# A gated scan and a routed expert layer on one core: scan rounds and matmul units in turns, sums of squares on TensorE, streamed expert weights

## The chip, the cores and the metric

The kernel runs on one core of a Trainium2 chip. The metric is the time of one execution in microseconds (us) on the device; the median of several runs is compared.

## What is computed

The reference has two parts. The first is a gated linear recurrence for 4 batches x 8 heads, 768 steps, head size 48, with a complex state of 48 x 48 per head:

```python
mag = np.sqrt(a_re * a_re + a_im * a_im)
scale = np.minimum(mag, 0.999) / (mag + 1e-06)
...
for t in range(S):
    new_re = ar * S_re - ai * S_im
    new_im = ar * S_im + ai * S_re
    S_re, S_im = (new_re + k_t v_t^T, new_im)
    y[:, :, t] = q_t S_re
```

Its output, 3072 rows of 384, is the input of the second: a layer of 8 experts where each row goes to the one expert with the largest logit (`x @ w_gate` plus a bias by modality), and is scaled by that expert's probability:

```python
h = np.maximum(x[mask] @ w1[e], 0.0)            # 384 -> 1024
out[mask] = gate_w[mask, None] * (h @ w2[e])    # 1024 -> 384
```

## The kernel before

The 768 steps are cut into 8 blocks of 96 steps. Batch, head and block together are 256 chains; 128 of them lie on the 128 partitions, so there are two **rounds** (two batches each).

`elem(r)` scans a round on VectorE, backwards in time, in 12 chunks of 8 steps. `A` holds the products of the gates from a step to the block's end; a step is two dependent instructions, `x<-A,an` (L132) and `A<-x` (L135). `norm` makes the gates `an` of a chunk: squares on ScalarE (L63), their sum on VectorE (`m`, L66), logarithm and exponentials on ScalarE, then `g` (L73) and `an` (L76) on VectorE. `hats` divides by the products: squares of `A` (L90), their sum on VectorE (`me`, L93), logarithm and exponential, then `qc`, `Qh` and `A*kc` on VectorE; `Qh` is turned by TensorE (`tq`, L107) into `QT`, and the scaled keys go to DRAM as `kh`. Both are generators whose pieces are written between the steps of the scan. `A` and `QT` have one buffer each.

`units(r)` has 16 units, 8 blocks x 2 batches. A unit loads `kh` and `v` (from ScalarE's DMA queue), turns the keys (`tk`, L170), multiplies them with `QT` (`wp`, L176), masks the product on VectorE (`KW`, L177), and makes state and output (`py`, L191 and L195). From block 1 on, the state of the block before is first multiplied by the block's decay (`t1`, `t2`, `Z`, L154 to L157, both batches at once). Then come the router's logits (`lg_ps`, L204), and the output goes as bfloat16 rows to DRAM (`x_rows`).

The program runs `elem(0)`, `units(0)`, `elem(1)`, `units(1)`, in this order of writing. Each engine has one in-order queue; the framework's scheduler sets its order when the kernel is built, and may move an instruction ahead where its inputs and buffers are ready.

`moe_sorted` then casts all weights to bfloat16 into SBUF (16 DMAs on POOL's queue, L253 and L254), makes the routing (logits, largest, rank within the expert, position in a list of slots: a chain on VectorE, with 64 small matmuls into `inv_ps`, L370), and runs 31 slot tiles of 128 rows. A tile belongs to one expert, whose number is read into a register of TensorE (`texp`). It gathers its rows (`xg`, indirect DMA on POOL's queue), turns them (`xg_ps`, L386), multiplies up (`h_ps`, L395, 24 matmuls), applies the rectifier on VectorE and ScalarE (`hT`), multiplies down (`y_ps`, L403, 8 matmuls), scales (`y_sb`) and scatters (`out_dram`, L406). The lines where the register stands in an address:

```python
te = nc.values_load(texp[0:1, i:i + 1], engines=[ET.PE], min_val=0, max_val=E - 1, ...)
...
nc.tensor.matmul(h_ps[:, f, :], w1s[:, bass.ds(te, 1), k, ff * 128:(ff + 1) * 128], xgT[:, k, :], ...)
...
nc.tensor.matmul(y_ps[:], hT[:, f, :], w2s[:, bass.ds(te, 1), f, :], ...)
```

Of the kernel before, what the change touches and what calls it, by code (L numbers as in the profile page):

```python
# [22 lines left out]
def gate_loop(nc, ctx, tc, cpool, ident, identb, q, k, v, a_re, a_im, wgp, x_rows, lg):  # L23
# [10 lines left out]
    T = 8  # L34

# [12 lines left out]
    def rows(x, r):  # L48
        return x[r * NB:(r + 1) * NB].rearrange("b h (g t) d -> (b h g) t d", t=L)

    def planes(x, n):
        return x[:, None].broadcast_to([P, 2, n, D])

    for_round = []

    def norm(r, c, box):

        t0 = c * T
        ab = st.tile([P, 2, T, D], F32, name="ab")
        nc.sync.dma_start(out=ab[:, 0], in_=rows(a_re, r)[:, t0:t0 + T])  # L60
        nc.sync.dma_start(out=ab[:, 1], in_=rows(a_im, r)[:, t0:t0 + T])
# [12 lines left out]
        yield  # L74
        an = st.tile([P, T, 4, D], F32, name="an", bufs=3)
        nc.vector.tensor_tensor(an[:, :, 0:2, :].rearrange("p t c d -> p c t d"), ab[:], planes(g, T), Alu.mult)  # L76
# [4 lines left out]
    def hats(r, c, A, QT):  # L81

        t0 = c * T
        qc = st.tile([P, T, D], F32, name="qc")
        kc = st.tile([P, T, D], F32, name="kc")
        nc.sync.dma_start(out=qc[:], in_=rows(q, r)[:, t0:t0 + T])
        nc.sync.dma_start(out=kc[:], in_=rows(k, r)[:, t0:t0 + T])
        e = A[:, t0 + 1:t0 + T + 1]
        sq = st.tile([P, T, 2, D], F32, name="sqe", tag="sq")
        nc.scalar.activation(sq[:], e, Act.Square)  # L90
# [9 lines left out]
        nc.vector.tensor_tensor(Qh[:], e, qc[:, :, None, :].broadcast_to([P, T, 2, D]), Alu.mult)  # L100
        yield
        nc.vector.tensor_tensor(e, e, kc[:, :, None, :].broadcast_to([P, T, 2, D]), Alu.mult)
        nc.sync.dma_start(out=kh[r, :, t0:t0 + T], in_=e.rearrange("p t c d -> p t (c d)"))
        for t4 in range(0, T, 4):
            tp = ps.tile([C, 4, P], F32, name="tq", tag="tp", bufs=2)
            for i in range(4):
                nc.tensor.transpose(tp[:, i, :], Qh[:, t4 + i].rearrange("p c d -> p (c d)"), ident[:])  # L107
            nc.scalar.copy(QT[:, :, t0 + t4:t0 + t4 + 4], tp.rearrange("c t p -> c p t"))  # L108

    def elem(r):  # L110
        A = qt.tile([P, L + 1, 2, D], F32, name="A")
        QT = qt.tile([C, P, L], F32, name="QT")
        for_round.append(QT)
        nc.vector.memset(A[:, L, 0, :], 1.0)
        nc.vector.memset(A[:, L, 1, :], 0.0)
        box = {}
        last = L // T - 1
        for c in (last, last - 1):
            for _ in norm(r, c, box):
                pass  # L120
        for c in range(last, -2, -1):

            hs = hats(r, c + 1, A, QT) if c < last else iter(())
            ns = norm(r, c - 2, box) if c > 1 else iter(())
            beside = [ns, hs, ns, hs, hs, ns, hs, hs, ns]
            next(ns, None)
            next(hs, None)
            if c >= 0:
                an = box.pop(c)
                for t in range(c * T + T - 1, c * T - 1, -1):  # L130
                    x = st.tile([P, 2, 2, D], F32, name="x")
                    nc.vector.tensor_tensor(x[:], A[:, t + 1, :, None, :].broadcast_to([P, 2, 2, D]), an[:, t - c * T].rearrange("p (u w) d -> p u w d", u=2), Alu.mult)  # L132
                    if beside:
                        next(beside.pop(0), None)
                    nc.vector.tensor_tensor(A[:, t], x[:, 0], x[:, 1], Alu.add)  # L135
            for g in (ns, hs):
                for _ in g:
                    pass
        nc.sync.dma_start(out=c_scr[r], in_=A[:, 0].rearrange("p c d -> p (c d)"))

    def units(r):
        QT = for_round[r]
        khv = kh[r].rearrange("(b h g) t c -> b g t h c", h=H, g=G)
        cv = c_scr[r].rearrange("(j u g) c -> u g j c", u=2, g=G)
        state = None
        for g in range(G):
            if g:
                cB = un.tile([P, NB * J, 2, D], F32, name="cB")
                for u in range(2):
                    nc.scalar.dma_start(out=cB[u * 64:(u + 1) * 64].rearrange("p j c d -> p j (c d)"), in_=cv[u, g][None].broadcast_to([64, NB * J, C]))  # L150
                t1 = un.tile([P, NB * J, 2, D], F32, name="t1", bufs=1)
                t2 = un.tile([P, NB * J, 2, D], F32, name="t2", bufs=1)
                Z = un.tile([P, NB * J, 2, D], F32, name="Z", bufs=1)
                nc.vector.tensor_tensor(t1[:], state[:], cB[:, :, 0:1, :].broadcast_to([P, NB * J, 2, D]), Alu.mult)  # L154
# [67 lines left out]
    for r in range(NR):  # L222
        units(r)
        if r + 1 < NR:
            elem(r + 1)
# [252 lines left out]
```

## Time and profile before

| what | before |
|---|---|
| runs, median of 3 | 863.29 us (860.55 to 863.85) |
| profiled execution | 852.87 us |
| its span, first to last instruction | 851.2 us |
| mean granted TensorE clock | 0.735 |
| TensorE busy | 581.7 us (68%) |
| VectorE busy | 360.2 us (42%) |
| ScalarE busy | 280.2 us (33%) |
| GpSimd (POOL) busy | 82.8 us (10%) |
| DMA, bytes and mean rate | 71.58 MB, 84 GB/s |

A busy time is the union of an engine's instructions. TensorE's matmuls are pipelined, so a busy TensorE may still wait inside; the distance from one matmul to the next tells more. PE is TensorE's matmuls, PEld its loads of the stationary operand, PEclk the share of the full clock that was granted (1.00 or 0.50 in any one moment). In the first 130 us the clock column shows 1.00 although the distances between matmuls are those of the low level; the distances are used there. A DMA share over 1 stands for engines that were full all the time.

### The profile page before, as it was taken

How to read it: one execution, taken by the hardware profiler on the slowest of the kernel's cores; microseconds unless marked ns; L12 is line 12 of the kernel's file. 1: busy time of each engine (PE TensorE's matmuls, PEld its weight loads, DVE VectorE, ACT ScalarE, POOL GpSimd, SP SyncE). 2: the span in 40 equal slices, each digit the busy share in tenths (PEclk: the TensorE clock that was granted, in tenths of full speed). 3: DMA queues.
4: the chain of work that ended last, by engine and by line, in shares of the span. 5: the costliest groups of instructions: out<-in, count | busy, mean ns of one | idle time of the engine just before them, and what ended most of it. 6: DMA issues, size and time to landing. Idle time of an engine off the chain costs nothing. (4 is left out here: it accounts for less than half of the span.)

```text
span 851.2 us, 11577 instructions
## 1 busy us (share of the span) xinstructions
PE 581.7 (68%) x3599; PEld 367.9 (43%) x3599; DVE 360.2 (42%) x835; ACT 280.2 (33%) x620; POOL 82.8 (10%) x122
## 2 busy tenths in 40 slices
PE   0122128998889712299998930179999999999996
PEld 0121125766666512166776720164444444444443
DVE  5999971256767999523334320700111101111110
ACT  6766542253645874333434310001111111111111
POOL 0000000000000000000000032021212212122110
PEclk9999999967977955567879975555665656566665
DMA  4434343342532542433334169960110101111000
GB/s 140 140 116 144 111 132 85 69 105 68 130 105 86 160 146 90 118 79 78 82 77 95 29 94 207 208 115 29 33 39 29 42 29 33 39 29 42 11 1 1
DMA packets 104774, 71.58 MB, mean 84 GB/s; under 512 B 72878, under 2 KB 96930, under 8 KB 104720
## 3 DMA queue, kind: packets, MB, share of 16 engines
q0 software_dynamic: 14992, 20.36, 11.8%
q1 hardware_dynamic: 24768, 30.82, 11.8%
q10 hardware_dynamic: 64960, 19.67, 10.5%
q8 instruction: 35, 0.57, 0.3%
q14 instruction: 19, 0.16, 0.1%
HBM read 66.79 MB, written 17.99 MB: 100 GB/s over the span
## 5 line engine op out<-in xcount | busy, mean ns | idle before, releaser
L395 PE MATMUL h_ps<-xgT,w1s 128*128 128x128 bf16 x744 | 169.5, 250 | 20.2 <-DVE xgT L388 14.5
L107 PE MATMUL tq<-ident,Qh 128*96 128x128 f32 x192 | 42.6, 397 | 151.7 <-DVE Qh L100 150.9
L395 PEld LDWEIGHTS <-w1s 128*128 x744 | 76.5, 103 | 118.0 <-issue 42.9
L107 PEld LDWEIGHTS tq<-ident,Qh 128*96 128x96 f32 x192 | 32.3, 184 | 161.2 <-issue 78.9
L400 ACT ACTIVATE hT<-h_ps 128x512 bf16<-128x512 f32 x31 | 18.5, 597 | 236.1 <-PE h_ps L395 236.1
L191 PE MATMUL py<-KW,V 96*64 96x192 f32 x512 | 82.3, 405 | 7.4 <-issue 7.3
L177 DVE TENSOR_TENSOR KW<-wp,mask 96x384 f32<-96x384 f32 x64 | 35.3, 553 | 120.3 <-PE wp L176 119.2
L403 PE MATMUL y_ps<-w2s,hT 128*128 x248 | 83.8, 515 | 0.0
L388 DVE COPY xgT<-xg_ps 128x384 bf16<-128x384 bf16 x31 | 11.1, 358 | 150.6 <-PE xg_ps L386 150.6
L176 PE MATMUL wp<-QT,KT 96*96 96x96 f32 x512 | 72.0, 305 | 2.1 <-ACT KT L171 1.9
L132 DVE TENSOR_TENSOR x<-A,an 128x192 f32<-128x192 f32 x192 | 68.2, 355 | 6.1 <-ACT an L78 1.8
L176 PEld LDWEIGHTS wp<-QT,KT 96*96 96x96 f32 x512 | 64.0, 212 | 12.2 <-ACT KT L171 5.4
L398 DVE TENSOR_SCALAR hT<-h_ps 128x512 bf16<-128x512 f32 x31 | 21.5, 692 | 91.8 <-PE h_ps L395 91.8
L164 POOL MEMSET V<- 96x128 f32 x32 | 6.4, 202 | 466.1 <-PE py L191 466.1
L135 DVE TENSOR_TENSOR A<-x 128x96 f32<-128x96 f32 x192 | 49.1, 255 | 4.4
L382 POOL DMA_INDIRECT xg<-x_rows,idg x31 | 30.3, 976 | 204.5 <-PE xg_ps L386 172.5
L403 PEld LDWEIGHTS <-hT 128*128 128x128 bf16 x248 | 35.1, 146 | 31.9 <-issue 31.3
L170 PE MATMUL tk<-ident,KW 96*96 96x96 f32 x256 | 40.3, 298 | 10.9 <-DMA KW<-kh 10.5
L191 PEld LDWEIGHTS py<-KW,V 96*64 96x64 f32 x512 | 39.5, 167 | 18.5 <-issue 15.1
L195 PE MATMUL py<-QT,Zs 96*48 96x96 f32 x448 | 47.4, 285 | 0.0
L108 ACT COPY QT<-tq 96x512 f32<-96x512 f32 x48 | 27.5, 583 | 47.0 <-PE tq L107 44.0
L201 ACT COPY yT<-py 128x192 f32<-128x192 f32 x64 | 20.5, 320 | 65.9 <-DVE state L200 60.9
(115 smaller groups left out, 745.5 us busy)
## 6 DMA issues: line engine op xcount, KB each, us to landing
kh<-A SPq DMA_DIRECT2D x24, 384.0 KB, 2.9
KW<-kh ACTq DMA_DIRECT2D x32, 288.0 KB, 3.2
w1s<-in_moe_w_dram POOLq DMA_DIRECT2D x8, 768.0 KB, 27.5
w2s<-in_moe_w_dram POOLq DMA_DIRECT2D x8, 768.0 KB
cB<-c_scr ACTq DMA_DIRECT2D x28, 192.0 KB, 3.8
ab<-in_a_re_dram SPq DMA_DIRECT2D x24, 192.0 KB, 2.4
V<-in_v_dram ACTq DMA_DIRECT2D x32, 144.0 KB, 2.9
ab<-in_a_im_dram SPq DMA_DIRECT2D x24, 192.0 KB, 2.5
```

Source lines behind the costliest of these rows:

```text
L107: nc.tensor.transpose(tp[:, i, :], Qh[:, t4 + i].rearrange("p c d -> p (c d)"), ident[:])
L108: nc.scalar.copy(QT[:, :, t0 + t4:t0 + t4 + 4], tp.rearrange("c t p -> c p t"))
L132: nc.vector.tensor_tensor(x[:], A[:, t + 1, :, None, :].broadcast_to([P, 2, 2, D]), an[:, t - c * T].rearrange("p (u w) d -> p u w d", u=2 ...
L135: nc.vector.tensor_tensor(A[:, t], x[:, 0], x[:, 1], Alu.add)
L170: nc.tensor.transpose(tp[:, i, :], KW[:, h4 + i, 0:C], ident[:L, :L])
L176: nc.tensor.matmul(wp[:, i, :], KT[:, h4 + i, :], QT[:, p, :], start=True, stop=True)
L177: nc.vector.tensor_tensor(KW[:, h4:h4 + 4, C:], wp[:], mask[:, None, :].broadcast_to([L, 4, L]), Alu.mult)
L191: nc.tensor.matmul(py[u * 64:(u + 1) * 64, i, :], V[:, 2 * j + u, :], KW[:, 2 * j + u, :], start=True, stop=(g == 0))
L195: nc.tensor.matmul(py[u * 64:u * 64 + D, i, C:], Zs[:, j, u * 64:u * 64 + D], QT[:, p, :], start=False, stop=True)
L382: nc.gpsimd.indirect_dma_start(out=xg[:], out_offset=None, in_=x_rows_dram, in_offset=bass.IndirectOffsetOnAxis(ap=idg[:, i:i + 1], axis=0))
L395: nc.tensor.matmul(h_ps[:, f, :], w1s[:, bass.ds(te, 1), k, ff * 128:(ff + 1) * 128], xgT[:, k, :], start=(k == 0), stop=(k == KD - 1))
L403: nc.tensor.matmul(y_ps[:], hT[:, f, :], w2s[:, bass.ds(te, 1), f, :], start=(f == 0), stop=(f == NF - 1))
```

## The change

- **Scan.** The products are kept per chunk (`e`, three buffers) in place of the whole of `A`; `QT` has two buffers. `total` adds the two planes of squares on TensorE, by two float32 matmuls with the identity into the same PSUM tile, and ScalarE's logarithm reads PSUM: VectorE's `m` and `me` are gone. `norm` is cut into `modulus` and `gates`.
- **Turns.** `elem` and `units` are generators; the 13 turns of `elem(1)` are written between the 16 units of `units(0)`. A unit's first half (`front`) is written ahead of the second half (`back`) of the unit before.
- **Units.** `wp` is made in two halves of 64 output rows; the logits go to four column groups and are added by a matmul with `pairsum`; the decay is done per batch; the DMAs of a unit are issued from SP.
- **Weights.** 16 cast DMAs on POOL's queue bring the weights as bfloat16 to DRAM (`w1b`, `w2b`), one per turn of the scan, each waiting for that turn's last step.
- **Experts.** 19 slot tiles of 256 rows. SP reads the expert's number and streams its weights into one of three buffers; TensorE's addresses are fixed. The next tile's transposes stand between the up and the down part. The scatters no longer wait for each other.

```diff
+    def total(x, y):
+        out = ps.tile([P, T, D], F32, name="total", tag="wp", bufs=2)
+        nc.tensor.matmul(out[:], ident[:], x, start=True, stop=False)
+        nc.tensor.matmul(out[:], ident[:], y, start=False, stop=True)
+        return out[:]
...
-        nc.vector.tensor_tensor(m[:], sq[:, 0], sq[:, 1], Alu.add)
-        nc.scalar.activation(m[:], m[:], Act.Ln, scale=1.0 / (0.999 * 0.999))
+        nc.scalar.activation(m[:], total(sq[:, 0], sq[:, 1]), Act.Ln, scale=1.0 / (0.999 * 0.999))
...
-        nc.vector.tensor_tensor(m[:], sq[:, :, 0], sq[:, :, 1], Alu.add)
-        nc.scalar.activation(m[:], m[:], Act.Ln)
+        nc.scalar.activation(m[:], total(sq[:, :, 0], sq[:, :, 1]), Act.Ln)
...
-        QT = qt.tile([C, P, L], F32, name="QT")
+        QT = qt.tile([C, P, L], F32, name="QT", bufs=2)
...
+                if casts and (r or c < last - 1):
+                    cast = casts.pop(0)()
+                    tc.add_manual_dep(cast.ins, done.ins.name, ...)
...
-                        nc.tensor.matmul(wp[:, i, :], KT[:, h4 + i, :], QT[:, p, :], start=True, stop=True)
+                    for u in range(2):
+                        nc.tensor.matmul(wp[u * 64:(u + 1) * 64, i, :], KT[:, h4 + i, u * 64:(u + 1) * 64], QT[:, p, :], start=True, stop=True)
...
-                    nc.tensor.matmul(lg_ps[:, b, :], wgp[:, j, :], yT[:, j, :], start=(j == 0), stop=(j == J - 1))
+                nc.tensor.matmul(lg_ps[j * 32:(j + 1) * 32, b, :], wgp[:, j, :], yT[:, j, :], start=True, stop=True)
...
-    elem(0)
-    for r in range(NR):
-        units(r)
-        if r + 1 < NR:
-            elem(r + 1)
+    for _ in elem(0):
+        pass
+    for r in range(NR):
+        us = units(r)
+        if r + 1 < NR:
+            es = elem(r + 1)
+            n, m = NB * G, NCH + 1
+            done = 0
+            next(es)
+            for i in range(n):
+                next(us)
+                while done * n < (i + 1) * (m - 1):
+                    next(es)
+                    done += 1
...
+    def fetch(i):
+        te = nc.values_load(texp[0:1, i:i + 1], engines=[ET.SP], min_val=0, max_val=E - 1, ...)
+        w1t = fp.tile([128, KD, F], BF16, name="w1t")
+        w2t = fp.tile([128, NF, Dt], BF16, name="w2t")
+        nc.sync.dma_start(out=w1t[:], in_=w1b[bass.ds(te, 1)].rearrange("e p k f -> p (e k) f"))
+        nc.sync.dma_start(out=w2t[:], in_=w2b[bass.ds(te, 1)].rearrange("e p c d -> p (e c) d"))
...
+                    nc.tensor.matmul(h_ps[:, f, :], w1t[:, k, ff * 128:(ff + 1) * 128], xgT[:, k, :], start=(k == 0), stop=(k == KD - 1))
...
+                nc.tensor.matmul(y_ps[:], hT[:, f, s * 128:(s + 1) * 128], w2t[:, f, :], start=(f == 0), stop=(f == NF - 1))
...
+            tc.declare_no_dep(sc.ins, group="scatter", reason="rows of different tokens")
...
+    got = fetch(0)
+    xgT = turn(got[2])
     for i in range(NS):
+        coming = fetch(i + 1) if i + 1 < NS else None
+        hT = up(got[0], xgT)
+        if coming:
+            xgT = turn(coming[2])
+        down(i, got[1], hT)
+        got = coming
```

How the change moves instructions shows at three places. First TensorE's queue where one expert tile ends and the next begins (ISA is a register operation); before:

```order
L403 LDWEIGHTS hT
L403 ISA
L403 MATMUL y_ps<-w2s,hT 128x384
L386 LDWEIGHTS xg
L386 MATMUL xg_ps<-identb,xg 128x128
L383 TENSOR_LOAD texp
L395 ISA
L395 LDWEIGHTS w1s
L395 ISA
L395 MATMUL h_ps<-xgT,w1s 128x128
```

and in the change, where an up part ends, with the transposes of the next tile and the first down matmul (one of each kind):

```order
L477 LDWEIGHTS w1t
L477 MATMUL h_ps<-xgT,w1t 128x256
L465 LDWEIGHTS xg
L465 MATMUL xg_ps<-identb,xg 128x128
L489 LDWEIGHTS hT
L489 MATMUL y_ps<-w2t,hT 128x384
```

The read of the expert's number and the register operations are gone from this queue, and a matmul into `h_ps` has 256 columns.

Second VectorE's queue in the middle of round 0's units, where `state` and `Z` are the units' and the others the scan's; before:

```order
L132 TENSOR_TENSOR x<-A,an 128x192
L135 TENSOR_TENSOR A<-x 128x96
L177 TENSOR_TENSOR KW<-wp,mask 96x4x96 x2
L73 SCALAR_TENSOR_TENSOR g<-m,g 128x384
L200 TENSOR_TENSOR state<-Z,py 128x192
L97 TENSOR_TENSOR qc<-qc,me 128x384
L76 TENSOR_TENSOR an<-ab,g 128x2x8x48
L200 TENSOR_TENSOR state<-Z,py 128x192
L100 TENSOR_TENSOR Qh<-A,qc 128x768
L177 TENSOR_TENSOR KW<-wp,mask 96x4x96
L102 TENSOR_TENSOR A<-A,kc 128x768
L66 TENSOR_TENSOR m<-sq 128x384
```

and in the change:

```order
L155 TENSOR_TENSOR e<-x 128x96
L237 TENSOR_TENSOR state<-Z,py 128x192
L148 TENSOR_TENSOR x<-e,an 128x192
L237 TENSOR_TENSOR state<-Z,py 128x192
L109 TENSOR_TENSOR qc<-qc,me 128x384
L206 TENSOR_TENSOR t_1655<-state,cB 128x384
L112 TENSOR_TENSOR Qh<-e,qc 128x768
L207 TENSOR_TENSOR t_1656<-state,cB 128x384
L119 TENSOR_TENSOR e<-e,kc 128x768
L208 TENSOR_TENSOR Z<-t_1655,t_1656 128x4x48
```

Here `state` stands between the two halves of a step of the scan, which queues behind `py` on TensorE. The last step of the second scan stands behind 14 of the 16 units of round 0; before, six of its chunks stood behind the last unit.

Third POOL's queue around the routing (`io`, `idp`, `pref` are constants that the routing reads); before:

```order
L253 DMA w1s<-in_moe_w_dram 128x3x1024
L254 DMA w2s<-in_moe_w_dram 128x8x384
L258 IOTA io_4339 128x128
L260 IOTA idp_4341 96x32
L262 IOTA pref 96x8
L275 AFFINE_SELECT trib<-trib 128x128
L320 IOTA thr 128x24
L382 DMA xg<-x_rows,idg 128x384 x6
```

and in the change:

```order
L182 MEMSET KT 96x8x32
L179 MEMSET V 96x8x16 x2
L331 IOTA io_4901 128x128
L333 IOTA idp_4903 96x32
L335 IOTA pref 96x8
L337 IOTA thr 128x12
L348 AFFINE_SELECT trib<-trib 96x96
L457 DMA xg<-x_rows,idg 128x384 x10
L496 DMA out_dram<-y_sb,ids 3072x384 x2
```

The casts stand far ahead, eleven of them before the first unit's mask and five between the units' memsets.

## Rows read from the trace of the kernel before

**Rows 1.** Windows: start:end, length, busy PE PEld DVE ACT POOL, clock, DMA share, GB/s.

```profile
0.00:130.00 130.00, 23.04 (x97) 17.55 (x98) 109.73 (x285) 75.68 (x135) 1.36 (x10) 1.00 0.44 133
130.00:285.00 155.00, 140.49 (x1123) 104.59 (x1124) 86.61 (x195) 73.92 (x196) 3.23 (x16) 0.85 0.36 89
285.00:361.00 76.00, 20.68 (x106) 15.54 (x104) 65.32 (x164) 42.72 (x81) 0.00 (x0) 0.56 0.45 133
361.00:498.00 137.00, 126.26 (x1128) 95.42 (x1126) 46.22 (x84) 50.93 (x146) 2.63 (x13) 0.83 0.30 71
498.00:570.00 72.00, 15.02 (x69) 14.15 (x69) 20.09 (x47) 0.42 (x1) 17.40 (x25) 0.50 1.07 178
570.00:846.00 276.00, 256.18 (x1082) 120.68 (x1082) 32.19 (x61) 36.44 (x62) 57.19 (x58) 0.61 0.10 28
```

**Rows 2.** Timeline of one expert tile, TensorE: start, length in us, line, operation, count.

```profile
649.86 5.73 PE L395 MATMUL h_ps<-xgT,w1s 128*128 128x128 bf16 x24 [0.45 <-DVE xgT L388]
655.39 0.42 PE L386 MATMUL xg_ps<-identb,xg 128*128 128x128 bf16 x2
655.60 2.76 PE L403 MATMUL y_ps<-w2s,hT 128*128 x8
```

**Rows 3.** Windows of two short stretches, for their clock (columns as in rows 1).

```profile
655.60:658.40 2.80, 2.80 (x11) 1.32 (x10) 0.00 (x0) 0.60 (x1) 0.00 (x0) 0.50 0.00 0
...
407.40:409.10 1.70, 1.70 (x21) 1.70 (x22) 0.59 (x2) 0.66 (x2) 0.00 (x0) 1.00 0.46 115
```

**Rows 4.** Line 395: TensorE's sequencer, durations in ns (min/median/max).

```profile
L395 PEldq FUSED_REGOPS  x1488: 46/55/60, 569.8 to 842.5; - x186
```

**Rows 5.** Timeline, TensorE: the same 16 passes of wp in two units.

```profile
362.15 2.88 PE L176 MATMUL wp<-QT,KT 96*96 96x96 f32 x16
...
407.47 1.55 PE L176 MATMUL wp<-QT,KT 96*96 96x96 f32 x16
```

**Rows 6.** The page's DMA part: mean rate; the SP queue (packets, MB, share of 16 engines).

```profile
DMA packets 104774, 71.58 MB, mean 84 GB/s; under 512 B 72878, under 2 KB 96930, under 8 KB 104720
...
q1 hardware_dynamic: 24768, 30.82, 11.8%
```

**Rows 7.** Timeline of the routing, VectorE and POOL; in brackets the idle time before.

```profile
534.80 0.49 DVE L302 SCALAR_TENSOR_TENSOR cand<-sh,pref 96x256 f32<-96x256 f32 x1 [24.42 <-POOL pref L262]
...
565.87 1.04 POOL L382 DMA_INDIRECT xg<-x_rows,idg  x1 [30.75 <-DVE empty L376]
567.21 0.98 POOL L382 DMA_INDIRECT xg<-x_rows,idg  x1 [0.30 <-issue]
```

**Rows 8.** Groups by line, TensorE: count, then busy us and mean ns of one.

```profile
L191 PE MATMUL py<-KW,V 96*64 96x192 f32 x512 | 82.3, 405 | 7.4 <-issue 7.3
L176 PE MATMUL wp<-QT,KT 96*96 96x96 f32 x512 | 72.0, 305 | 2.1 <-ACT KT L171 1.9
...
L204 PE MATMUL lg_ps<-yT,wgp 128*8 128x96 f32 x256 | 37.7, 280 | 4.0 <-ACT yT L201 3.0
```

**Rows 9.** Timeline of the first scan, VectorE: first and last step, and two adds' neighbours.

```profile
12.78 0.26 DVE L135 TENSOR_TENSOR A<-x 128x96 f32<-128x96 f32 x1
...
17.30 0.56 DVE L66 TENSOR_TENSOR m<-sq 128x384 f32<-128x384 f32 x1
17.78 0.55 DVE L73 SCALAR_TENSOR_TENSOR g<-m,g 128x384 f32<-128x384 f32 x1
...
118.26 0.26 DVE L135 TENSOR_TENSOR A<-x 128x96 f32<-128x96 f32 x1
```

**Rows 10.** Timeline, TensorE: last transposes of the first scan, first of the units.

```profile
122.86 1.91 PE L107 MATMUL tq<-ident,Qh 128*96 128x128 f32 x8 [6.33 <-DVE Qh L100]
...
129.92 1.49 PE L170 MATMUL tk<-ident,KW 96*96 96x96 f32 x8 [5.14 <-DMA KW<-kh]
```

**Rows 11.** Window of the casts (columns as in rows 1).

```profile
499.00:537.00 38.00, 0.63 (x2) 0.18 (x2) 5.09 (x16) 0.42 (x1) 14.18 (x21) 0.50 1.18 193
```

**Rows 12.** Timeline, TensorE: the last two matmuls.

```profile
844.63 0.84 PE L403 MATMUL y_ps<-w2s,hT 128*128 x2
```

More of the change, by code (lines that the diff above doesn't have):

```diff
@@ L127, in elem @@
             next(hs, None)
+            next(ms, None)
+            beside = [None, hs, ms, hs, hs, ms, hs, ms]
             if c >= 0:
                 an = box.pop(c)
-                for t in range(c * T + T - 1, c * T - 1, -1):
+                if c:
+                    E[c - 1] = st.tile([P, T, 2, D], F32, name="e", bufs=3)
+                for i in range(T - 1, -1, -1):
                     x = st.tile([P, 2, 2, D], F32, name="x")
[L132 to L135, printed above, removed]
@@ L136, in elem @@
-            for g in (ns, hs):
+                    nc.vector.tensor_tensor(x[:], E[c][:, i, :, None, :].broadcast_to([P, 2, 2, D]), an[:, i].rearrange("p (u w) d -> p u w d", u=2), Alu.mult)
+                    if i == T - 1:
+                        if c:
+                            gates(c - 1, box)
+                    else:
+                        next(beside[T - 1 - i], None)
+                    to = E[c][:, i - 1] if i else (E[c - 1][:, T - 1] if c else cl[:])
+                    done = nc.vector.tensor_tensor(to, x[:, 0], x[:, 1], Alu.add)
@@ L137, in elem @@
+                if casts and (r or c < last - 1):
+                    cast = casts.pop(0)()
+                    tc.add_manual_dep(cast.ins, done.ins.name, mybir.DependencyInfo(mybir.DependencyClass.Sync, mybir.DependencyReason.DATA), reason="spreads the casts over the turns")
+            for g in (ms, hs):
                 for _ in g:
                     pass
-        nc.sync.dma_start(out=c_scr[r], in_=A[:, 0].rearrange("p c d -> p (c d)"))
+            if c == 0:
+                nc.sync.dma_start(out=c_scr[r], in_=cl.rearrange("p c d -> p (c d)"))
@@ L222, in gate_loop @@
+        order = [(g, b) for g in range(G) for b in range(NB)]
+        made = front(*order[0])
+        for w, (g, b) in enumerate(order):
+            Z = decay(g, b) if g else None
+            ahead = front(*order[w + 1]) if w + 1 < len(order) else None
+            back(g, b, *made, Z)
+            made = ahead
+            yield
+    for _ in elem(0):
+        pass
     for r in range(NR):
-        units(r)
+        us = units(r)
         if r + 1 < NR:
-            elem(r + 1)
-def moe_sorted(nc, ctx, tc, cpool, ident, identb, lg, x_rows_dram, moe_modality_id, moe_modality_bias, moe_w1, moe_w2, out):
+            es = elem(r + 1)
[7 more added lines that the diff above has]
+                    done += 1
+            for _ in es:
+                pass
+        for _ in us:
+            pass
@@ new lines, in cast_weights @@
+def cast_weights(nc, moe_w1, moe_w2):
+    E, Dt, F = moe_w1.shape
+    w1b = nc.dram_tensor("w1b", (E, 128, Dt // 128, F), BF16, kind="Internal").ap()
+    w2b = nc.dram_tensor("w2b", (E, 128, F // 128, Dt), BF16, kind="Internal").ap()
+    casts = []
+    for e in range(E):
+        casts.append(lambda e=e: nc.gpsimd.dma_start(out=w1b[e], in_=moe_w1[e].rearrange("(k p) f -> p k f", p=128)))
+        casts.append(lambda e=e: nc.gpsimd.dma_start(out=w2b[e], in_=moe_w2[e].rearrange("(c p) d -> p c d", p=128)))
+    return w1b, w2b, casts
```

388 lines of the change are left out of this document (206 added, 182 removed).

## The prediction

> **What bounds the kernel now.** I read the stretches of the span first [rows 1], then single instructions inside each. The rows show five stages with different limits. Stage A, the scan of round 0 (0 to 130): VectorE 109.73 us busy of 130, TensorE 23. Stage B (130 to 361): the units of round 0, with part of the scan of round 1 between them until 285, and the rest of that scan alone until 361, where TensorE is busy 20.68 of 76 us. Stage C (361 to 498): the units of round 1, TensorE busy 126.26 of 137 at a mean granted clock of 0.83. Stage D (498 to 570): routing, with no engine busy for long and the DMA engines full. Stage E (570 to 846): 31 expert tiles, TensorE busy 256.18 of 276 at 0.61. What a change is worth has to be asked of each stage by itself.
>
> Stage E is busy but not fast. A tile has 24 matmuls into h_ps in 5.73 us, 0.24 each, and 8 into y_ps in 2.76 us, 0.32 to 0.35 each [rows 2]. The y matmuls stream 384 columns, which is 0.32 us at 1.2 GHz, the level that their stretch shows (0.50) [rows 3]. The h matmuls stream only 128 columns and should take a third of that, 0.107. What they wait for is TensorE's own sequencer: 1488 register operations for 744 matmuls, two each of 55 ns [rows 4], since every address of w1s contains the expert number. So 24 matmuls cost 5.7 us where the columns ask for 2.6.
>
> **The change, stage by stage.** *E, expert tiles.* Now 19 tiles of 256 slots with fixed addresses. Per tile the up part streams 24 x 256 columns, the down part 16 x 384, and 6 transposes stream 128. At 0.32 us per 384 columns [rows 2, 3] that is 24 x 0.213 + 16 x 0.32 + 6 x 0.107 = 10.9 us at 1.2 GHz, and half, 5.4 us, at 2.4 GHz. Rows of the same wp matmuls show that the level matters as much as that: 16 passes take 2.88 us in one place and 1.55 in another, where the clock is 1.00 [rows 3, 5]. Three other resources have to keep up. SP streams 1.57 MB of weights per tile: the SP queue moved 30.82 MB in 11.8% of the span, 100 us, so 307 GB/s [rows 6], 5.1 us per tile. Gathers and scatters: 31 pairs took a DMA share of 0.10 of 276 us [rows 1], 0.9 us a pair, two pairs a tile, 1.8 us; together 6.9, less if the 6 KB pieces of a weight row move faster than that queue's mean packet of 1.2 KB. POOL issues four indirect DMAs, 1.3 us apart [rows 7], 5.2 us. The evictions (one more hT pair and a second y_sb) are shared by VectorE and ScalarE, which were busy 32 and 36 of 276 us [rows 1]; they are free as long as TensorE needs over 4 us a tile. I take 6.6 us, between TensorE's 5.4 and the DMA's 6.9 and nearer to the DMA: 19 x 6.6 = 125 us for 276. Bounds: 105 (5.5 a tile) and 207 (10.9).
>
> By a rule of the Trainium skill (TensorE: Matmul & The Clock Gate, "HAM oscillation") bursts of matmuls that wait for a transfer between them start each time at the low level. The trace agrees as far as it goes: after the idle stretch of routing the clock stands at 0.50 [rows 1]. Were it to hold here, the sum would have 207 and not 125; that is rival 1.
>
> *D, routing.* VectorE waits 24.42 us for an iota that stands on POOL's queue behind the 16 casts of the weights [rows 7]. With the casts gone from there, this wait goes. The first tile needs two gathers (+1.3) and a wider transpose and copy (+0.7 by the 0.42 us for two transposes [rows 2]); the index matrices grow from 32 to 38 columns, under 1 us. 72 - 24.4 + 2 = 50 us. What is late next is the DVE chain itself; the first weight tiles load under it.
>
> *C, units of round 1.* wp becomes two passes of 64 output rows side by side. Bounds: nothing, if they overlap, up to another 36 us a round (half of the 72.0 busy) if they don't. I take nothing: py already runs in such halves, and streams 192 columns in 0.161 us of busy time a pass where wp needs 0.141 for 96 [rows 8]. lg_ps moves to four column groups: it costs 37.7 us in 32 units, 1.2 each [rows 8]; between 0 and three quarters of that are saved, I take half, 0.5 after the extra switch. The decay of the state is now done per batch, four small VectorE instructions twice in place of four large ones; that is off TensorE's path. The DMA issues move from ScalarE's queue to SP's, behind kh, x_rows and the loads there; KW has three buffers to cover it. A unit costs 137 / 16 = 8.6 us, at clock 0.83 as much as 7.1 us at full level; 16 x (7.1 - 0.5) / 0.83 = 127, I take 130.
>
> *B, round 0's units with round 1's scan.* QT has two buffers now and the scan's chunks alternate with the units from the start, so the 76 us with the scan alone go. TensorE per unit, in full-level time: 6.6 as above; 6 transposes of Qh (96 / 16; eight took 1.91 us at the low level [rows 10], so 0.21 each there and 0.11 at the full one), 0.65; and the new sums of squares. Such a sum is two float32 matmuls of 384 columns, each in two passes; a pass of 96 columns takes 1.55 / 16 = 0.097 [rows 5], so 384 take 0.36 to 0.39 and the sum 1.4 us (2.6 to 2.9 at the low level). 24 a round, 1.5 a unit: 2.1 us. Total 9.35, at the 0.85 of this stage [rows 1] 11.0 us, 16 x 11.0 = 176. VectorE needs less: 12 chunks of 8.8 us (from 12.78 to 118.26 [rows 9]) less the two adds, 0.48 apart [rows 9], so 94, and 46 to 50 for its work in the units (stage C's row), 144. In-order queues on both sides cost something; I take 184 for 231. Bounds 144 and 231.
>
> *A, scan of round 0.* Per chunk VectorE loses two adds, 0.96 us, of which 0.15 comes back since they filled the gap between dependent steps: 8.0 us. But two sums now run in series on TensorE before ScalarE's logarithm: at full level that hides, at the low level 2.4 us of 5.2 stand out, 10.4 a chunk. TensorE's share of a chunk lies between the two uses at which I saw either level, so I take the middle, 9.2, where 8.8 was. Before the first step add 1.6, behind the last 2: 14 + 110 + 13.4 = 137 for 130 (first tk at 129.92 [rows 10]). Bounds 125 and 152. Eleven of the 16 casts also run here. They filled all 16 engines for 38 us with nothing beside them (share 1.18 [rows 11]), so 11 take some 26 to 45 us of a stage that already uses 0.44 of 130 [rows 1]. I cost them at nothing because loads are a chunk ahead; without that cover it is rival 2.
>
> The Trainium skill (DMA: Bandwidth & Descriptors, "Issuing engines are not separate DMA queues") says that transfers from all three issuing engines run on the same 16 engines and interleave. No row here shows casts beside loads; by it 0.44 becomes 0.7 to 0.8 and the loads still fit.
>
> **Sum.** 137 + 184 + 130 + 50 + 125, and 6 behind the last y matmul (845.5 [rows 12] to 851.2): 632 against the span of 851.2. The profiled execution took 852.87, the runs 863.29 in the median, 1.2% more; so 632 + 1.7, times 1.012, is **640 us**.
>
> **Rivals.** *1: TensorE stays at 1.2 GHz in the expert tiles*, since it waits for weights in every tile. For: 0.61 in stage E now; against: 16 y matmuls and 24 h matmuls back to back, with nothing on its queue between them. 19 x 10.9 = 207, +82 and times 1.012: 723 us. *2: the alternation doesn't pay*: VectorE's in-order queue waits for py and the sums, TensorE's for KW and Qh, and the casts delay loads. Stage B takes its old 231 and A its 152, +62 and times 1.012: 703 us. *3: slower than before*: the weight stream itself is the bound. It decides from (863 / 1.012 - 1.7 - 507) / 19 = 18.1 us a tile, 87 GB/s; at 84 GB/s, the mean that this program's DMA moved [rows 6], a tile takes 18.7 and the total is 875 us. For it: the load of one tile hangs on a register that SP reads first, and on buffers that TensorE frees; against: three buffers, and 307 GB/s on that queue.
>
> **How the numbers follow.** Forecast 0.62 (its own range 590 to 690: below, stage B at 144 and 5.5 us a tile; above, some six tenths of either rival's price), rival 1 0.20, rival 2 0.14, rival 3 0.03, and 0.01 that all of it cancels. The range of 8 in 10 is 592 to 725: it takes in the centres of rivals 1 and 2. Half a per cent is about what a measurement of this kernel can tell from no change; faster by more 0.96, within 0.01, slower 0.03.
>
> **What would show it.** Right: no register operations in front of the expert matmuls, h_ps at about 0.11 us and a clock near 1.0 there, 19 tiles 6 to 7 us apart; VectorE's wait of 24 us for pref gone; the last step of the second scan before the last unit of round 0, and no stretch of tens of us with TensorE idle between the rounds. Wrong: TensorE waiting for w1t or w2t in each tile, matmuls at 0.21 us; VectorE waiting in each chunk for me or m behind the sums of squares, chunks over 10 us; ab or qc landing late while casts run.

## The result, and the profile after

The changed kernel takes 598.39 us in the median of four runs (596.78 to 604.11), against 862.02 before (the median of four, three of which gave the 863.29 further up): a ratio of 0.695, 95% interval 0.690 to 0.700. Forecast were 640 us, with 592 to 725 for eight times in ten, so the result lies inside the range and near its lower end. The profiled execution took 597.93 us with a span of 596.2, so here the profile stands for the median as it is.

The stages as windows, changed kernel (columns as in [rows 1]): scan of round 0, turns, units of round 1, routing, expert tiles.

```profile
0.00:145.00 145.00, 76.35 (x206) 40.80 (x207) 108.81 (x283) 80.89 (x150) 9.72 (x21) 0.73 0.78 178
145.00:316.00 171.00, 156.37 (x1580) 106.67 (x1578) 132.06 (x344) 107.97 (x262) 12.84 (x38) 0.96 0.70 162
316.00:433.00 117.00, 109.42 (x1384) 82.01 (x1384) 48.17 (x112) 49.05 (x141) 7.18 (x28) 0.96 0.42 86
433.00:477.00 44.00, 17.42 (x96) 15.54 (x91) 19.84 (x46) 2.00 (x7) 5.06 (x10) 0.54 0.34 117
477.00:590.00 113.00, 108.05 (x868) 80.99 (x867) 48.02 (x75) 33.71 (x57) 69.57 (x71) 0.98 0.86 296
```

| stage | before | forecast | after | miss |
|---|---|---|---|---|
| A, scan of round 0 | 130 | 137 | 145 | +8 |
| B, round 0's units with round 1's scan | 231 | 184 | 171 | -13 |
| C, units of round 1 | 137 | 130 | 117 | -13 |
| D, routing | 72 | 50 | 44 | -6 |
| E, expert tiles | 276 | 125 | 113 | -12 |

The stages sum to 36 us below the forecast. The step of 1.2% from the profile to the median, which was not there, adds 7.6 us, and 1.3 us of that are gone again because 633.7 x 1.012 is 641.3 and was written as 640: together the 42 us by which the forecast was too high.

An expert tile, timeline of TensorE in the changed kernel (columns as in [rows 2], which it answers).

```profile
495.47 2.78 PE L477 MATMUL h_ps<-xgT,w1t 128*128 128x256 bf16 x24
498.09 0.50 PE L465 MATMUL xg_ps<-identb,xg 128*128 128x128 bf16 x6
498.43 2.76 PE L489 MATMUL y_ps<-w2t,hT 128*128 128x384 bf16 x16
```

Twice the columns of [rows 2] go through h in half the time: 24 matmuls of 256 columns in 2.78 us where 24 of 128 took 5.73, and no register operation stands before them. With the clock at 0.98 the next tile begins 5.55 us later, TensorE's own time (forecast 5.4 for TensorE and 6.6 for the tile). After a first tile of 7.2 us twelve tiles run so. Then the lead of three tiles that the stream of weights had from the routing is used up. These are TensorE's waits in stage E (line waited for: us, times, longest):

```profile
PE h_ps L477 <- DMA w1t<-w1b: 2.4, 3, 1.8
PE y_ps L489 <- DMA w2t<-w2b: 1.9, 2, 1.4
```

Three late tiles take 7.6, 8.2 and 6.1 us, 5.2 more than three at the pace of the others. Over all 19 a tile took 5.9 us.

### The profile page after: what moved, and what is told of

It is laid out like the page before. It is cut to its first block, busy times and chain, and to the rows that moved or that the text cites. A ratio compares the mean times of both kernels' runs of the same rounds, so it can differ in the third digit from the quotient of the medians.

```text
span 596.2 us, 11093 instructions
## 1 busy us (share of the span) xinstructions
PE 467.6 (78%) x4124; PEld 326.0 (55%) x4124; DVE 356.9 (60%) x859; ACT 273.6 (46%) x615; POOL 105.3 (18%) x168
## 5 line engine op out<-in xcount | busy, mean ns | idle before, releaser
L148 DVE TENSOR_TENSOR x<-e,an 128x192 f32<-128x192 f32 x192 | 68.0, 354 | 4.3
L66 PE MATMUL total<-sqe,ident 128*128 128x384 f32 x48 | 27.4, 660 | 41.8 <-ACT sqe L103 41.8
L193 PE MATMUL wp<-QT,KT 96*64 96x96 f32 x1024 | 57.4, 264 | 2.4 <-ACT KT L187 1.3
L477 PE MATMUL h_ps<-xgT,w1t 128*128 128x256 bf16 x456 | 54.7, 278 | 2.4 <-DMA w1t<-w1b 2.4
L193 PEld LDWEIGHTS wp<-QT,KT 96*64 96x64 f32 x1024 | 50.7, 147 | 6.7 <-ACT KT L187 5.4
L489 PE MATMUL y_ps<-w2t,hT 128*128 128x384 bf16 x304 | 52.5, 326 | 1.9 <-DMA w2t<-w2b 1.9
L477 PEld LDWEIGHTS <-w1t 128*128 128x128 bf16 x456 | 45.3, 100 | 11.1 <-DMA w1t<-w1b 3.6
L155 DVE TENSOR_TENSOR e<-x 128x96 f32<-128x96 f32 x190 | 48.4, 255 | 4.9 <-DMA kh<-e 0.7
L496 POOL DMA_INDIRECT out_dram<-y_sb,ids x38 | 37.9, 996 | 26.8 <-ACT y_sb L492 17.3
L116 PE MATMUL tq<-ident,Qh 128*96 128x128 f32 x192 | 27.2, 288 | 14.8 <-DVE Qh L112 14.8
```

Of the source, the lines that this page charges most:

```text
L148: nc.vector.tensor_tensor(x[:], E[c][:, i, :, None, :].broadcast_to([P, 2, 2, D]), an[:, i].rearrange("p (u w) d -> p u w d", u=2), Alu.mult)
L155: done = nc.vector.tensor_tensor(to, x[:, 0], x[:, 1], Alu.add)
L193: nc.tensor.matmul(wp[u * 64:(u + 1) * 64, i, :], KT[:, h4 + i, u * 64:(u + 1) * 64], QT[:, p, :], start=True, stop=True)
L477: nc.tensor.matmul(h_ps[:, f, :], w1t[:, k, ff * 128:(ff + 1) * 128], xgT[:, k, :], start=(k == 0), stop=(k == KD - 1))
L489: nc.tensor.matmul(y_ps[:], hT[:, f, s * 128:(s + 1) * 128], w2t[:, f, :], start=(f == 0), stop=(f == NF - 1))
L496: sc = nc.gpsimd.indirect_dma_start(out=out, out_offset=bass.IndirectOffsetOnAxis(ap=ids[:, c:c + 1], axis=0), in_=y_sb[:], in_offset=None ...
```

## The experiments

They ran on four chips, so a total is compared with runs taken beside it on the same chip, before among them, and across chips the comparison goes stage by stage. The kernels of the first three experiments (experts of before, old gate, resident weights) ran once each. The stages are read from TensorE's instructions: A to the first transposed key (tk), B to the last xp of round 0, C to the last xp of all, E from the first h to the last y.

| kernel | A | B | C | E | median, us |
|---|---|---|---|---|---|
| changed kernel | 144.8 | 168.4 | 121.1 | 112.2 | 598.4 |
| changed kernel again | 144.5 | 173.2 | 120.6 | 115.0 | 603.7 |
| experts of before | 145.8 | 166.5 | 125.0 | 275.4 | 792.0 |
| resident weights | 142.1 | 175.5 | 121.3 | 160.1 | 685.8 |
| six buffers | 144.0 | 170.0 | 124.7 | 115.8 | 604.5 |
| adds on VectorE | 133.7 | 183.0 | 124.4 | 114.8 | 609.2 |
| unit first | 142.0 | 179.3 | 124.4 | 115.6 | 612.8 |
| casts late | 145.7 | 191.7 | 124.1 | 116.1 | 626.4 |
| one matmul for wp | 143.5 | 165.6 | 140.3 | 109.6 | 611.0 |
| mixed, casts beside last units | 133.4 | 165.8 | 154.2 | 111.0 | 621.9 |
| mixed, casts early | 134.3 | 168.1 | 124.8 | 116.0 | 588.0 |

Nearly the same code in the same stage differs by up to 9 us in B (166.5, where no casts run, to 175.5) and by 4 in A and in C from one run to another; less than that is read from no single row.

**Which half brings what.** First the new gate part with the experts of before (no casts to HBM, the resident weights loaded after the gate part):

```diff
-    moe_sorted(..., x_rows, w1b, w2b, ...)      # 19 tiles of 256, streamed
+    moe_sorted(..., x_rows, moe_w1, moe_w2, ...)  # as in the kernel before
```

> The changed gate part with the experts of before (resident weights, 31 tiles of 128, casts after the gate part). Theory (the gains of the two parts add up): the gate part ends at 433 as in the changed kernel, then the routing with its wait for the casts 72, 276 for the tiles and 6 behind: 787 us. Rival (the gate part only gained because nothing of the casts was behind it, or the experts' TensorE work was slow only because of the gate's state of the clock): the tile part is under 240 us and the time under 755.

792.0 us against 856.7 of before on that chip: the gate part alone is worth 65 us, and the expert part behind it took 275.4 us as before. Then the other way round:

```diff
-        gate_loop(..., lg, casts)
+        gate_loop(..., lg)      # as before, with one cast after each V memset of round 0
```

> The gate part of before, with one cast to HBM beside each unit of round 0, and the changed routing and experts. Theory: 498 for the gate part, then 44 and 112 and 7 as in the changed kernel: 661 us. Rival (the new experts profit from the busy TensorE that the new gate leaves behind): the tiles start at 1.2 GHz and stay there for a part, 20 to 100 us more, 680 to 760.

683.1 us. Routing and tiles took 43 and 115 as expected, with the clock at 1.0 from the fifth microsecond of the first tile; some 20 of the 22 us above the expectation are in the old gate part, which ended at 516 in place of 496: all 16 casts ran in its first 85 us (DMA share 1.15), and its first keys stood at 141 in place of 129.92 [rows 10]. The rivals fall: 65 us and 174 us make 239, of the 252 by which the changed kernel with six buffers (below) beat before on that chip, and neither half lives off the other's clock.

**Fixed address or larger tile.**

```diff
-        nc.sync.dma_start(out=w1t[:], in_=w1b[bass.ds(te, 1)]...)
-        ... nc.tensor.matmul(h_ps[:, f, :], w1t[:, k, ...], ...)
+        nc.sync.dma_start(out=w1s[:, e], in_=w1b[e])   # all experts, once
+        ... nc.tensor.matmul(h_ps[:, f, :], w1s[:, bass.ds(te, 1), k, ...], ...)
```

> The changed kernel with tiles of 256, but all weights resident in SBUF (loaded as bf16 during the routing) and addressed through a register on TensorE, as before. Theory (the fixed address is worth more than half of the tile's gain): matmuls stay 227 ns apart, a tile takes 24 x .227 + 16 x .227 = 9.1 us, 19 of them 173, against 112: 660 us. Rival (the tile of 256 alone brings it, since one address now covers 256 columns): tiles of 5.5 us, 104 in all without the waits for the stream, 590 us.

685.8 us, of which 36 are the load of all weights before the first tile (it begins at 517.1; at 481.3 in the repeated changed kernel). The tiles take 8.35 us. Sequencer and matmuls of line 478, and one tile's timeline:

```profile
L478 PEldq FUSED_REGOPS  x912: 2/55/717, 516.6 to 674.2; - x183
```

```profile
560.50 5.69 PE L478 MATMUL h_ps<-xgT,w1s 128*128 128x256 bf16 x24
566.03 0.50 PE L466 MATMUL xg_ps<-identb,xg 128*128 128x128 bf16 x6
566.36 2.76 PE L490 MATMUL y_ps<-w2s,hT 128*128 x16
```

The h part is back at 5.7 us, with two register operations of 55 ns for each matmul, one before its weight load and one before itself, and 0.227 us from one matmul to the next. What fills the rest of the 0.227 us is not shown. The y part is not slower at all, against my 16 x 0.227: there the address stands in the streamed operand, with one operation each, and 384 columns cover it. So of the 160 us by which stage E became shorter, the fixed address brings some 45 (160 to 115 in the repeated changed kernel). The other 115 (275 to 160) came with everything else that changed in this stage: the larger tile, the order of the queue, the scatters, and a granted clock of 0.97 here where it was 0.61 [rows 1]. These were not taken apart. The register operations are not what held the clock at 0.61, since here they are back and the clock stays at 0.97.

**Deeper buffers, and the changed kernel once more.** 

> Weight tiles in six buffers in place of three, nothing else. Theory (the stream is a little slower than TensorE and its lead of three tiles is used up by tile 13): three more tiles are fetched during the routing, the late tiles lose their 5.4 us, 593 us, ratio to before .688. Rival (the transfers slow each other, the stream has no spare rate before the tiles either): within 1 us of the changed kernel's 598.4.

```diff
-        w1t = fp.tile([128, KD, F], BF16, name="w1t")
+        w1t = fp.tile([128, KD, F], BF16, name="w1t", bufs=6)   # w2t likewise
```

The waits for weights are gone, and still E takes 115.8. The evictions of h start late, and so did those of the changed kernel with three buffers when it ran again (on another chip than the runs above, against what its text says):

> The changed kernel once more, beside the next three and on the chip of the first four. In the six-buffer run the evictions of h began up to 1.6 us after the matmul they wait for, while weights were on their way, and a tile took 6.05 us without any wait for weights; in the first run of the changed kernel they began 0.04 to 0.10 us after it, and a tile took 5.55 us, but late tiles waited for weights. If the buffers make the difference: tiles of 5.55 us again, 598 us. If chip or run make it: tiles of 6.05 us here too, about 602 us.

ScalarE's waits between 490 and 575 us, repeated changed kernel; in the first run of the same code only the first of these releasers occurs:

```profile
ACT hT L481 <- PE h_ps L477: 24.5, 12, 2.4
ACT hT L481 <- PE xg_ps L465: 21.7, 14, 2.2
```

The third and fourth eviction of most tiles began up to 1.6 us (2.0 in one first tile) after the matmul they needed had ended by the record, in both kernels, and in none of the last three tiles; a tile took 6.05 us. Kernels with streamed weights that ran together on one chip agreed in this: three chips gave 6.05 us, and a fourth, like the first result, 5.55. So it goes with the chip or the occasion and not with the buffers, 603.7 for 604.5 (0.706 and 0.707 of before), and six buffers bring nothing there. Whether they would help where the evictions are prompt was not seen.

**Sums of squares on VectorE.**

```diff
-        nc.tensor.matmul(out[:], ident[:], x, start=True, stop=False)
-        nc.tensor.matmul(out[:], ident[:], y, start=False, stop=True)
+        nc.vector.tensor_tensor(out, x, y, Alu.add)
```

> Sums of squares back on VectorE (an add into m), all else as in the changed kernel. Theory of the prediction (the adds cost VectorE .96 us a chunk more, TensorE has room): the first scan 12 x .5 to 1.1 longer, the turns no shorter, 604 to 612 us. Rival (the way through TensorE at its low level costs the waits for g and qc, 37 us in all, and in the turns TensorE, busy 156 of 171 us, is what bounds): the waits in the first scan shrink by 10 to 15 us more than the adds take, and 24 sums of 1.4 us leave TensorE in the turns: 565 to 590 us.

609.2 us, and both theories are half right: the first scan is shorter, as the rival has it, and the turns are not, as the theory has it. First transposed key and last scan steps (cl; first and last start), this kernel and then the repeated changed kernel:

```profile
L184 PE MATMUL tk<-ident,KW x256: 243/247/396, 133.7 to 431.2; 96*96 96x96 f32 x128
L153 DVE TENSOR_TENSOR cl<-x x2: 258/258/258, 119.3 to 306.8; 128x96 f32<-128x96 f32 x2
```

```profile
L186 PE MATMUL tk<-ident,KW x256: 243/246/396, 144.5 to 428.4; 96*96 96x96 f32 x128
L155 DVE TENSOR_TENSOR cl<-x x2: 252/254/257, 127.8 to 291.4; 128x96 f32<-128x96 f32 x2
```

In round 0 the adds on VectorE are 10.8 us better. VectorE's waits there in the changed kernel:

```profile
DVE g L84 <- ACT g L82: 15.5, 9, 9.0
DVE qc L109 <- ACT me L107: 13.1, 11, 5.4
```

With the adds on VectorE 8 us of such waits are left of these 29, and the adds cost less than that gain. In the turns the adds are 10 us worse: 183.0 us, and 165.6 to 175.5 in the eight profiles with turns where TensorE makes the sums, apart from the two that move the first unit or the casts. The window of the turns, with the adds on VectorE and in the repeated changed kernel:

```profile
134.00:322.00 188.00, 162.49 (x1516) 117.01 (x1516) 135.97 (x364) 111.39 (x263) 12.72 (x38) 0.77 0.65 150
```

```profile
145.00:320.00 175.00, 157.73 (x1579) 107.06 (x1577) 131.92 (x343) 107.85 (x262) 12.84 (x38) 0.95 0.67 157
```

TensorE has 24 sums fewer to do and is busy for longer, 162 us for 158, at a granted clock of 0.77 in place of 0.95. TensorE's wait for VectorE's `Qh` in these windows, adds on VectorE and repeated changed kernel:

```profile
PE tq L114 <- DVE Qh L110: 9.6, 6, 3.7
```

```profile
PE tq L116 <- DVE Qh L112: 1.9, 2, 1.3
```

The three stretches at the half level inside the turns (from 157, 212 and 249 us, 85 us in all) each begin at one of these waits. So two accounts stand side by side: the sums were work that kept the clock up, or VectorE, with 24 adds more, hands over `Qh` late and TensorE's clock falls in the gap. No run separates them.

**Which comes first at the start of the turns.**

```diff
-            next(es)
             for i in range(n):
                 next(us)
+                if i == 0:
+                    next(es)
```

> The first unit is written before the first turn of the second scan, where the changed kernel has the turn first. Theory (the 25.8 us from the last scan step of round 0 to the first transposed key are long because the second scan's first chunk stands ahead on ScalarE, VectorE and SP): 8 to 13 us of it go, 585 to 590 us. Rival (that chunk is only moved, and the turns, bound by TensorE, end as late): 596 to 600 us.

612.8 us, a miss on the far side of both. The first key is 2.5 us sooner, but the second scan ends later (297.8 for 291.4 in the repeated changed kernel) and the turns with it: B 179.3 against 173.2. VectorE now has the first unit's mask ahead of the second scan in its queue, and idles until the keys have come (first the scan's last steps, then the mask's row with the idle time before it):

```profile
L155 DVE TENSOR_TENSOR cl<-x x2: 249/254/259, 125.9 to 297.8; 128x96 f32<-128x96 f32 x2
145.05 0.55 DVE L194 TENSOR_TENSOR KW<-wp,mask 96x384 f32<-96x384 f32 x1 [10.84 <-PE wp L193]
```

**Where the casts stand.**

```diff
-                if casts and (r or c < last - 1):
+                for _ in range(2 if casts and r and c < last - 1 else 0):
```

> No cast in the first scan, two a chunk in the second. Prediction's term (casts cost nothing in the first scan): within 2 us of the changed kernel. Rival (the casts slow the loads of the first scan, chunks of 9.4 us go back to 8.7): the first scan ends 6 to 9 us sooner, 590 us; if twice the casts in the turns then delay the keys' loads there, it is lost again there.

626.4 us. A is as long without a cast as with the ten that run there (145.7 and 144.5), so casts, one a chunk, cost nothing there, as forecast. Two a chunk in the turns cost 18 us. VectorE's largest wait there (4.6 us in the repeated changed kernel) and the turns' window up to 312 us; the repeated changed kernel has a DMA share of 0.68 in the same window:

```profile
DVE e L155 <- DMA kh<-e: 17.5, 5, 4.6
```

```profile
145.00:312.00 167.00, 141.84 (x1320) 95.90 (x1322) 122.03 (x326) 94.70 (x226) 19.90 (x43) 0.88 0.96 193
```

The scan waits for its own keys to be written, since their buffer is free only then. One cast a chunk can't be told from none: B is 166.5 with none (experts of before) and 168 to 175 with six.

**No turns.**

```diff
-            next(es)
-            for i in range(n):
-                next(us)
-                while done * n < (i + 1) * (m - 1): ...
+            for _ in us:
+                pass
```

> Scan and units of round 0 and 1 one after another again, all else as in the changed kernel. Theory (in the turns TensorE's 7.3 us of a unit lie beside VectorE's 9 of a chunk): the units of round 0 take 16 x 7.3, the second scan 113, with the two ends between them 15 each, 260 us where the turns take 172: about 685 us. Rival (the turns pay little, as each side waits for the other, and the other edits shorten the stage): under 630 us.

669.7 us. Units of round 0, scan of round 1 alone, units of round 1:

```profile
141.00:261.00 120.00, 113.38 (x1404) 84.11 (x1405) 50.01 (x115) 52.38 (x149) 8.20 (x32) 0.95 0.43 87
261.00:391.00 130.00, 68.29 (x194) 37.61 (x194) 97.23 (x250) 68.23 (x127) 4.63 (x6) 0.71 0.58 140
391.00:509.00 118.00, 110.84 (x1398) 82.88 (x1396) 48.79 (x117) 50.55 (x145) 7.95 (x33) 0.96 0.39 83
```

Units and scan one after the other take 250 us where the turns take 171. That is rival 2 of the prediction, and it falls.

**One matmul for the masked scores.**

```diff
-                    for u in range(2):
-                        nc.tensor.matmul(wp[u * 64:(u + 1) * 64, i, :], KT[:, h4 + i, u * 64:(u + 1) * 64], ...)
+                    nc.tensor.matmul(wp[:, i, :], KT[:, h4 + i, 0:L], ...)
```

> The masked scores by one matmul of 96 rows, as before the change, in place of two halves of 64; all else as in the changed kernel. Prediction's term (the halves cost nothing): within 2 us of 603.7. Rival A (the second matmul is what keeps TensorE's granted clock at 1.0 in the last units): the clock there falls back to .83 and a unit takes 8.6 us, 20 us more. Rival B (the halves cost eight matmuls of .1 to .2 us a unit): 0.9 to 1.7 us a unit less in the 16 last units, 577 to 590 us.

The total is open: the runs lay between 598.5 and 616.2 us. The price of the halves is not. Groups of wp by line over the last 75 and 80 us of the units, at a clock of 1.0 (busy us, mean ns), repeated changed kernel and one matmul:

```profile
L193 PE MATMUL wp<-QT,KT 96*64 96x96 f32 x307 | 15.6, 248 | 0.0
```

```profile
L192 PE MATMUL wp<-QT,KT 96*96 96x96 f32 x158 | 15.7, 252 | 0.0
```

Twice the matmuls keep TensorE busy no longer: the halves run side by side, as forecast. With one matmul the clock stood at 1.0 for the last 95 us of the units, so it is not the halves that hold it there, and rival A falls in that form. Its 20 us did come in the profiled execution (611.2 us): C took 140.3 us, because the level stayed at 0.50 for 44 us behind a wait for keys at the stage's start. First TensorE's row behind that wait and the window, then the same of the repeated changed kernel, where it came back after 10 us:

```profile
312.40 1.49 PE L186 MATMUL tk<-ident,KW 96*96 96x96 f32 x8 [2.59 <-DMA KW<-kh]
312.00:356.00 44.00, 42.93 (x236) 31.30 (x238) 11.03 (x24) 11.08 (x33) 2.16 (x8) 0.50 0.25 54
```

```profile
320.90 1.49 PE L186 MATMUL tk<-ident,KW 96*96 96x96 f32 x8 [2.53 <-DMA KW<-kh]
320.20:330.40 10.20, 9.50 (x87) 8.60 (x89) 1.97 (x4) 1.90 (x4) 0.51 (x2) 0.50 0.30 56
```

The execution of 598.5 us has no room for 44 us at that level. Whether the halves bear on how long it lasts isn't settled.

**Towards a better version.** VectorE adds for round 0, TensorE for round 1; first with the last six casts moved beside the units of round 1:

```diff
+        if r == 0:
+            nc.vector.tensor_tensor(m, x, y, Alu.add)
+            return m
-                if casts and (r or c < last - 1):
+                if casts and r == 0 and c < last - 1:
+            if casts and r and w % 2 == 0:    # in units
+                cast = casts.pop(0)()
```

> Sums of squares on VectorE in round 0 and on TensorE in round 1; the casts that stood in the turns are put beside the units of round 1, every second one. From the two runs before: the first transposed key 10.8 us sooner, and six casts fewer in the turns, whose chunks took 13.5 us with a cast, 16 with two and 12.3 without: 7 to 10 us. Together 583 to 586 us on this chip. Rival (casts beside the last units delay the keys' loads there as they did in the turns): the last units 10 us longer, 593 us.

621.9 us, beyond both. A and B came as hoped, and C took 154 us for 121. Windows of stage C, then TensorE's waits for keys there, all of them and the longest:

```profile
300.00:320.00 20.00, 17.63 (x182) 14.30 (x182) 6.63 (x14) 6.53 (x21) 2.03 (x6) 0.74 0.48 87
320.00:345.00 25.00, 21.13 (x272) 15.72 (x270) 9.69 (x22) 9.73 (x28) 2.38 (x7) 0.95 0.87 157
345.00:365.00 20.00, 16.65 (x174) 12.83 (x171) 5.64 (x14) 6.08 (x18) 1.72 (x5) 0.76 0.58 110
365.00:421.00 56.00, 54.55 (x415) 41.45 (x412) 14.60 (x34) 14.34 (x39) 3.91 (x11) 0.50 0.46 84
421.00:455.00 34.00, 29.67 (x369) 20.84 (x367) 12.34 (x34) 14.33 (x42) 2.54 (x10) 1.00 0.46 79
```

```profile
PE tk L190 <- DMA KW<-kh: 7.1, 4, 2.5
364.33 0.53 PE L190 MATMUL tk<-ident,KW 96*96 96x96 f32 x2 [2.49 <-DMA KW<-kh]
```

In the repeated changed kernel TensorE waits 2.5 us for keys in this stage, once. Here it is four waits and 7.1 us; that is not 33. The rest is the clock: 56 us at half level with TensorE busy 54.55 of them, so some 27 us lost. The level fell at 363.2, inside the wait that ended at 364.33, and TensorE waited for no keys after that. The Trainium skill (TensorE: Matmul & The Clock Gate, "HAM oscillation") has waits for transfers between bursts of matmuls as a cause of the low level. The trace agrees as to the fall. But a wait of the same 2.5 us was followed by 10 us at the half level in the repeated changed kernel, by 44 with one matmul for wp and by 58 here, so the length of the wait alone does not set how long the level lasts; what does is open.

Last, twelve casts in the first scan and four in the turns, none beside the last units:

```diff
-                if casts and (r or c < last - 1):
+                if r == 0 or c in (2, 3, 4, 5):
```

> Sums of squares on VectorE in round 0 and on TensorE in round 1, as in the run before; of the casts, twelve in the first scan, one beside each chunk, and four in the turns beside chunks 5 to 2 of the second scan, none beside the last units. From the run before: first transposed key at 133.4 in place of 144.5; two casts fewer in the turns than in the changed kernel at 1.2 us each, the last units at 1.0 of the clock again: 603.7 - 11.1 - 2.5 = 590 us. Rival (a cast beside every chunk fills the DMA engines in the first scan: 5.2 + 3.8 us of their time for each chunk of 9.2): chunks over 9.7 us and nothing left of the gain, 600 us.

588.0 us in the median of seven runs, ratio to before 0.690 (0.686 to 0.694), where the changed kernel had 0.695 (0.690 to 0.700) and, again, 0.706 (0.700 to 0.712); against the first of these two the intervals overlap, so only against the second is it shown to be faster. The first key stands at 134.3, and the expert tiles here took 6.05 us. Ten of the 16 us below the repeated run are stage A's and shown; five in B lie within the scatter of that stage.

## Why the prediction was right, and where it was off

*Faster by much: right, and for the reasons given.* The four large terms were the expert tiles, the turns, the routing's wait and the clock. The first three are each borne out by a run or a row; the clock rose as forecast in stage E, 0.98 for 0.61, but no run shows what raised it. VectorE's 24 us for pref [rows 7] are gone from the routing, 44 us for 72:

```profile
440.15 0.42 DVE L372 SCALAR_TENSOR_TENSOR cand<-sh,pref 96x256 f32<-96x256 f32 x1
```

It came 6 under the forecast, and not because the added gathers and columns were cheap: from `cand` to the first gather it is 31.4 us (31.1 before), from there to the first h 5.7 (4.3), as forecast. What I had not seen is the load of the modality numbers (`mid`), which VectorE awaits ahead of `cand`: VectorE began behind it 2.9 us after the last xp, and 9.8 us before.

*A, "at the low level 2.4 us of 5.2 stand out": the one term with the wrong sign against its alternative.* I let VectorE's chunk get 0.96 shorter and took 9.2 us, the middle of 8.0 and 10.4. Steady chunks took 10.0 to 10.9 us in the changed kernel, at and above the upper end, though the clock in this stage was 0.73 and not at its low level throughout; so the term was too small, and the prediction's own sign of being wrong, VectorE waiting in each chunk behind the sums, did come: 13.1 us for qc and, beside 9.0 at the start, 6.5 for g. With the adds on VectorE chunks take 9.2 again, and A is 133.7, where before had 129.92 [rows 10]. Sums on TensorE cost this stage 11 us. Ten casts ran in this stage, not the eleven of the sum; at a cost of nothing that changes no term.

*B, 184 against 171: right mechanism, clock term mis-sized.* I divided TensorE's work by the 0.85 of the old stage [rows 1]; it became 0.96. With that the sum gives 16 x 9.35 / 0.96 = 156 us, and TensorE was busy for 156.37 of 171. That the clock would rise here was not foreseen. Without the sums of squares it was 0.77, but then TensorE also waits longer for `Qh`, so it is not shown that the sums keep it up.

*C, 130 against 117: the same step.* In time at the full level I forecast 6.6 us a unit; eight units took 58.3 us at level 1.0 in the repeated run (first wp to first wp, from 340.2 to 398.5), 7.3 each. The work was even undersized. What failed is the division by 0.83. In the old stage C TensorE's wait for keys was one of 5.3 us; it waited 4.3 us in seven pieces for the copied logits (`lgT`), and all four of the stage's falls to the half level came within 2.5 us behind such a piece, though not every piece was followed by one. In the changed kernel that wait is down to 0.2 us. Which of the edits keeps the level up was not tried: waits of 0.73 us for `Zs` are new there, and no fall follows them.

*E, 6.6 against 5.55 to 6.05 us for most tiles, 5.9 on average.* I went towards the DMA's 6.9, worked out from a mean rate of 307 GB/s [rows 6] and scatters beside it. The stream does need longer than TensorE, but a lead of three tiles from the routing covers thirteen tiles. Rival 1, a clock that stays low because the tiles wait for weights, did not come: few wait, and the clock is 0.98. Rival 3's bound lies far off, with 296 GB/s moved in this stage.

*The range's foot.* Stage B at 144 and 5.5 us a tile, which the prediction names for it, make 580 us by its own sum and not the 590 that it gives.

*The 1.2% from the profile to the median*: the profile of before was one of its shorter executions, that of after a middle one. A ratio of this kind from one execution should widen the range and not move the centre.

## What to carry to other kernels

Ask of every edit what it does to TensorE's granted clock in its stage: with 24 sums fewer TensorE was busy for longer, and behind one wait of 2.5 us the stage lost some 27 us more to the half level. An operation can belong on different engines in different stages: the sums are better on VectorE in the first scan, where TensorE is mostly idle (11 us, in three runs), and by the one run that tried it better on TensorE in the turns. Background transfers are free until a short-lived buffer waits for its own write or its own load, so put them where the slack is and not where the bytes seem few.

## What the runs showed of the hardware

- A register in the address of the loaded operand brings two sequencer operations of 55 ns a matmul and 0.227 us from one matmul to the next, at 128 columns [rows 2, 4] and at 256 alike (0.109 at 256 with a fixed address). In the streamed operand it is one, hidden under 384 columns: 0.163 us apart with it and without.
- The same expert code ran at 5.55 us a tile in one run and at 6.05 in another, where VectorE and ScalarE began the third and fourth eviction of most tiles 0.15 to 1.6 us after the record of the matmul they wait for (0.04 us in the first). Three chips showed the slower pace, a fourth and the first result the other; the cause is open.
- The granted clock fell to 0.50 at a wait of 2.5 to 2.6 us for keys and came back after 10 us in the changed kernel, after 44 us with one matmul for wp (TensorE busy 98% of them) and after 58 us in the mixed kernel (97% of 56); what sets the length is open.
